# Weight gradient stage: who issues the row loads, and when the 3.2 MB operand is loaded

## The chip, the cores and the metric

One core of a Trainium2 chip. The metric is the device time of one execution in microseconds (us); times are medians of fast runs, and every run told here was fast (the single-look run, being alone, is of unknown state). A profile is one execution, so its span differs a little from the median.

## The reference, cut to what matters

The program is the backward pass of a block that adds segmented attention, gated by an MLP, to its input. Only the gradient of the attention weights Wq, Wk, Wv and of the attention's input concerns us here:

```python
q = jnp.einsum('btd,dhe->bhte', h, Wq)      # also k, v; 32 heads of 128, D = 640
scores = jnp.einsum('bhqe,bhke->bhqk', q, k) * scale
p = _softmax(jnp.where(mask, scores, -1e9))
o = jnp.einsum('bhqk,bhke->bhqe', p, v)
...
_out, _vjp = jax.vjp(_f, ...)               # gradients of all weights and of x
```

64 segments of 32 tokens and 8 memory tokens are handled three at a time: 22 units ("tl") of up to 120 rows.

## The kernel before: the parts concerned

The stage makes eight passes ("qd") over the 22 units, 512 weight columns a pass. For one unit it loads dS, P and the rows of output gradient ("g"), q and k. TensorE forms the three gradient blocks in PSUM (`s2`), ScalarE or VectorE copies them out, and `s4` multiplies them by the weights (the g matmuls, line 1390). After the 22 units, `wg` multiplies them by the layer's input rows `hr` (line 1411).

```python
def ld(u):                                        # five units ahead: NB = 5 buffers
    nc.sync.dma_start(dS[0:n], ...)
    nc.sync.dma_start(Pr[0:n], ...)
    for nm_ in ("g", "q", "k"):
        k.load_x(r, 0, src, nc.scalar if nm_ == "g" else nc.sync)   # token rows
        k.load_m(r, tl, nm_, c0, c0 + 512, nc.gpsimd)               # memory-token rows
...
def s2(u, i):
    ... four matmuls into pr ...
    if i == 0:   nc.scalar.copy(gr[0:n], pr[0:n])                   # line 1351
    elif i == 1: nc.vector.tensor_scalar(gr[0:n], pr[0:n], k.scale, ...)
    else:        nc.scalar.activation(gr[0:n], pr[0:n], ACT.Copy, scale=k.scale)   # line 1355
...
ld_to(2)
ld_w(0)                                           # three transposing weight loads, SyncE
ld_to(3)
nc.scalar.dma_start(hr[0:120], k.HRO[...])        # 3000 KB
nc.scalar.dma_start(hr[120:P], k.HRO[...])        # 200 KB
ld_to(5)
...
for qd in range(8):
    for p in range(NTL):                          # 22 units
        ...ld_to(u + 2 + NB); s2(u + 2, ...); s1(u + 3); s3(u + 1, ...); s4(u)
        if p == 4:
            spill(qd)                             # three loads gr<-GSP, 160 KB each, GpSimd
    ...
    for i in range(3):
        wg(qd, i)                                 # first reader of hr
```

In the traces of this stage ScalarE, SyncE and GpSimd run their instructions in the order in which the program wrote them. A DMA issue is one of these instructions; where one had to wait, what stood behind it in the same engine's queue waited too (8.46 us in the prediction's example). Two counts are in use below: the units that are loaded count from 0, as in the code, the places of the edits from 1 ("the seventh unit" is `u == 6`).

Of the kernel before, what the change touches and what calls it, by code (L numbers as in the profile page):

```python
# [16 lines left out]
P = 128  # L17
# [1247 lines left out]
def phase6_Awgrads(k, X, out0, out3, out4, out5):  # L1265

    nc, tc = k.nc, k.tc
# [4 lines left out]
    NF = NTL - 2  # L1272
# [5 lines left out]
    with tc.tile_pool(name="h6i", bufs=3) as io, tc.tile_pool(name="h6", bufs=1) as hp, \  # L1278
            tc.tile_pool(name="h6g", bufs=1) as gp, tc.tile_pool(name="h6a", bufs=1, space=bass.MemoryType.PSUM) as pa:
        start = len(nc.cur_bb.bb.instructions)  # L1280
        hr = hp.tile([P, NF, D], BF16, name="hr")
# [26 lines left out]
        def ld(u):  # L1308
            qd, tl = units[u]
            c0, h0 = qd * 512, qd * 4  # L1310
            ns, nm, nx, n = k.geo(tl)
            dS, Pr = dSs[u % NB], Prs[u % NB]
            nc.sync.dma_start(dS[0:n], k.DSR[tl][:, h0:h0 + 4, :])
            nc.sync.dma_start(Pr[0:n], k.PR[tl][:, h0:h0 + 4, :])
            rw = []
            for nm_ in ("g", "q", "k"):
                r = io.tile([120, 512], BF16, name="r6", tag=f"r6{nm_}", bufs=NB)
                src = k.g_src(tl, c0, c0 + 512) if nm_ == "g" else k.x_src(tl, nm_, c0, c0 + 512)
                k.load_x(r, 0, src, nc.scalar if nm_ == "g" else nc.sync)
                k.load_m(r, tl, nm_, c0, c0 + 512, nc.gpsimd)  # L1320
                rw.append(r)
            st["l", u] = (dS, Pr, rw)

        def ld_to(u):
            while cnt["l"] < min(u, len(units)):
                ld(cnt["l"])
                cnt["l"] += 1

        def s1(u):
            n = k.geo(units[u][1])[3]  # L1330
            dS = st["l", u][0]
            pt = pa.tile([P, 4, n], BF16, name="t6", tag=bank("x", 5, 3))
            for j in range(4):
                nc.tensor.transpose(pt[:, j, :], dS[0:n, j, 0:P], k.ident[0:n, 0:n])  # L1334
            nc.vector.tensor_copy(dSTs[u % 2][0:n, :, 0:n], pt[0:n])  # L1335

        def s2(u, i):
            qd, tl = units[u]
            n = k.geo(tl)[3]
            dS, Pr, rw = st["l", u]  # L1340
            lh = (Pr, dS, dSTs[u % 2])[i]
            pr = pa.tile([P, 512], F32, name="r6p", tag=bank("s", 3, 2))
            for j in range(4):
                nc.tensor.matmul(pr[:, j * P:(j + 1) * P], lh[0:n, j, :], rw[i][0:n, j * P:(j + 1) * P],  # L1344
                                 start=True, stop=True)
            if tl < NF:
                gr = grs[i][:, tl, :]
            else:
                gr = gp.tile([120, 512], BF16, name="grs", tag=f"grs{i}", bufs=2)[:]
            if i == 0:  # L1350
                nc.scalar.copy(gr[0:n], pr[0:n])  # L1351
            elif i == 1:
                nc.vector.tensor_scalar(gr[0:n], pr[0:n], k.scale, None, op0=ALU.mult)
            else:
                nc.scalar.activation(gr[0:n], pr[0:n], ACT.Copy, scale=k.scale)
            st["g", u, i] = gr
            if tl >= NF:
                r0 = 120 * (tl - NF)
                nc.gpsimd.dma_start(k.GSP[qd, i, r0:r0 + n, :], gr[0:n])  # L1359
            if i == 2:  # L1360
                st.pop(("l", u))

        def spill(qd):
            for i in range(3):
                nc.gpsimd.dma_start(grs[i][120:P, :, :], k.GSP[qd, i].rearrange("(t r) c -> r t c", r=8))

        def s3(u, i0, i1):
            qd, tl = units[u]
            nx = k.geo(tl)[2]
            a = (96 * tl) % R if tl < NF else R + 96 * (tl - NF)  # L1370
            pt = pa.tile([P, i1 - i0, 4, nx], BF16, name="t6g", tag=bank("x", 5, 3))
            for i in range(i0, i1):
                gr = st.pop(("g", u, i))
                for j in range(4):
                    nc.tensor.transpose(pt[:, i - i0, j, :], gr[0:nx, j * P:(j + 1) * P], k.ident[0:nx, 0:nx])  # L1375
            k.copy(ring[:, i0:i1, :, a:a + nx], pt[:], eng='s' if i1 == 2 else 'v')

        def s4(u):
            qd, tl = units[u]
            if tl < NF:  # L1380
                ws = [(w, P * (w % 3)) for w in range((96 * tl) // P, (96 * tl + 96) // P)]
            else:
                ws = [(NT - 1, R)] if tl == NF + 1 else []
            for w, r0 in ws:
                g = []
                for h in range(2):
                    pg = pa.tile([P, 320], F32, name="g6", tag=bank("g", 0, 3))
                    for i in range(3):
                        for j in range(4):
                            nc.tensor.matmul(pg[:], ring[:, i, j, r0:r0 + P], Ws[qd][i][:, j, 320 * h:320 * h + 320],  # L1390
                                             start=(i == 0 and j == 0), stop=(i == 2 and j == 3))
                    g.append(pg)
                gx = io.tile([P, D], BF16, name="gxo", tag="wgo", bufs=4) if qd == 7 else None
                for h in range(2):
                    a = acc[:, w, 320 * h:320 * h + 320]
                    if qd == 0:
                        nc.vector.tensor_copy(a, g[h][:])
                    else:
                        nc.vector.tensor_tensor(a if qd < 7 else gx[:, 320 * h:320 * h + 320], a, g[h][:], ALU.add)  # L1399
                if qd == 7:  # L1400
                    nc.sync.dma_start(k.GXA[P * w:P * w + P, :], gx[:])
# [16 lines left out]
        def out_ld(tt):  # L1418
            st["o"] = []
            for nm_, src in (("s", k.SR), ("g", k.GB), ("x", k.A_x)):  # L1420
                t_ = io.tile([P, D], BF16, name=f"eo_{nm_}", tag=f"eo_{nm_}", bufs=1)
                nc.gpsimd.dma_start(t_[:], src[tt * P:tt * P + P, :])
                st["o"].append(t_)

        def out_rows(tt):
            s, g, x = st.pop("o")
            nc.vector.tensor_tensor(g[:], s[:], g[:], ALU.mult)
            nc.vector.tensor_tensor(g[:], g[:], x[:], ALU.add)
            nc.gpsimd.dma_start(out0f[tt * P:tt * P + P, :], g[:])
# [16 lines left out]
        ld_to(2)  # L1446
        ld_w(0)
        ld_to(3)
        nc.scalar.dma_start(hr[0:120], k.HRO[0:120 * NF, :].rearrange("(t p) d -> p t d", p=120))
        nc.scalar.dma_start(hr[120:P], k.HRO[120 * NF:k.NR, :].rearrange("(t r) d -> r t d", r=8))  # L1450
        ld_to(5)
        for _ in head(0):
            pass
        for qd in range(8):
            u0 = NTL * qd
            for p in range(NTL):
                u = u0 + p
                if p + 2 < NTL:
                    ld_to(u + 2 + NB)
                    s2(u + 2, 0)  # L1460
                    s2(u + 2, 1)
                if p + 3 < NTL:
                    s1(u + 3)
                if p + 1 < NTL:
                    s3(u + 1, 0, 2)
                if p + 2 < NTL:
                    s2(u + 2, 2)
                if p + 1 < NTL:
                    s3(u + 1, 2, 3)
                s4(u)  # L1470
                if p == 4:
                    spill(qd)
                if p % 11 == 2:
                    out_ld(2 * qd + p // 11)
                if p % 11 == 6:
                    out_rows(2 * qd + p // 11)
            if qd < 7:
                ld_w(qd + 1)
                h = head(u0 + NTL)
            else:  # L1480
                xg = X.tile([P, NW * (D + 512)], BF16, name="xg", tag="x")
                gow = xg[:, 0:NW * D].rearrange("p (t d) -> p t d", d=D)
                orr = xg[:, NW * D:NW * (D + 512)].rearrange("p (t d) -> p t d", d=512)
                h = NW // 2
                for a in range(2):
                    rows = slice(h * P * a, h * P * (a + 1))
                    nc.scalar.dma_start(gow[:, h * a:h * a + h, :], k.GWO[rows, :].rearrange("(t p) d -> p t d", p=P))
                    nc.sync.dma_start(orr[:, h * a:h * a + h, :], k.OR[rows, 0:512].rearrange("(t p) c -> p t c", p=P))
            for i in range(3):
                wg(qd, i)  # L1490
                if qd < 7:
                    next(h)
# [337 lines left out]
def kernel(  # L1830
# [42 lines left out]
    with tc.tile_pool(name="xw", bufs=1) as X:  # L1873
        wo_ops = phase6_Awgrads(k, X, out_0, out_3, out_4, out_5)
        phase5_Bbwd_ln(k, X, *wo_ops, out_1, out_6, out_7, out_8, out_9)
# [35 lines left out]
```

## Time and profile before

| | before |
|---|---|
| median, range | 5483.78 us, 5476.4 to 5496.66 (3 runs when the prediction was made; with a fourth, 5476.62, the median is 5480.2) |
| span of the profiled run | 5474.2 us |
| TensorE busy | 88% of the span |
| the stage (end of the chain before it to the end of the last wg) | 1420 us |

Busy time and share of each engine, from the page, then TensorE's work in the first and second pass (columns: window, its length, TensorE busy and its matmuls, granted clock, share of the DMA engines busy, GB/s):

```profile
PE 4830.6 (88%) x66012; PEld 3050.2 (56%) x66012; DVE 2297.2 (42%) x7285; ACT 1752.0 (32%) x4913; POOL 1558.4 (28%) x2673
...
3424.00:3553.00 129.00, 93.09 (x993) 0.82 0.70 160
3624.00:3725.00 101.00, 89.92 (x983) 0.95 0.64 156
```

The first pass has about the same work as the second, yet takes 28 us longer. A pass of 101 us leaves TensorE idle for 11. Whatever is to be gained in this stage lies in those differences, and in the time for which the clock is below 1. The waits behind them stand in the prediction.

### The profile page before, as it was taken

The numbers are of one execution on the slowest core, as the hardware profiler recorded it, in microseconds if no ns is written. First come the engines' busy times: TensorE is split into PE (matmuls) and PEld (weight loads), VectorE is DVE, ScalarE is ACT, GpSimd is POOL, SyncE is SP. The second block draws the span as 40 slices with busy tenths as digits, with TensorE's granted clock in tenths as the row PEclk, the third lists the DMA queues.
The fourth block names the chain that finished last, engine by engine and source line by source line (L and its number), as shares of the span: only waits on it lengthen the run. The fifth ranks groups of instructions, "written<-read, shape, count | busy, mean of one in ns | idle before, by whom it ended". The sixth has DMA issues, their size and how long they took to land. (4 is left out here: it accounts for less than half of the span.)

```text
span 5474.2 us, 163087 instructions
## 1 busy us (share of the span) xinstructions
PE 4830.6 (88%) x66012; PEld 3050.2 (56%) x66012; DVE 2297.2 (42%) x7285; ACT 1752.0 (32%) x4913; POOL 1558.4 (28%) x2673
## 2 busy tenths in 40 slices
PE   4988899989999785999999998789998999999999
PEld 2544555555555443555666665555566555666665
DVE  5833555555555423444444443322233222311451
ACT  2422455555555422232333332222233222301111
POOL 0000334343444212333333332432344333310100
PEclk9998999999999787999999999899999999999999
DMA  7553455555544587666766664744355444657332
GB/s 248 177 188 91 134 154 159 154 159 156 159 154 149 131 190 156 175 185 173 194 182 179 185 184 111 164 113 96 96 134 124 111 106 97 167 178 184 111 111 94
DMA packets 1004358, 822.92 MB, mean 150 GB/s; under 512 B 507009, under 2 KB 892333, under 8 KB 1000929
## 3 DMA queue, kind: packets, MB, share of 16 engines
q1 hardware_dynamic: 758779, 559.22, 37.2%
q0 software_dynamic: 95696, 155.10, 10.3%
q10 hardware_dynamic: 149130, 98.17, 6.5%
q8 instruction: 521, 8.54, 0.7%
q14 instruction: 232, 1.90, 0.1%
HBM read 476.95 MB, written 303.09 MB: 142 GB/s over the span
## 5 line engine op out<-in xcount | busy, mean ns | idle before, releaser
L1411 PE MATMUL wg<-gr,hr 128*128 128x512 bf16 x2400 | 529.4, 382 | 16.1 <-DVE dST L1335 12.9
L1390 PE MATMUL g<-w,ghacc 128*128 128x320 bf16 x3072 | 456.8, 307 | 0.0
L1411 PEld LDWEIGHTS <-hr 128*128 128x128 bf16 x2400 | 235.5, 98 | 301.5 <-issue 27.3
L1390 PEld LDWEIGHTS <-ghacc 128*128 128x128 bf16 x3072 | 301.9, 100 | 120.1
L308 PEld LDWEIGHTS <-hx 128*32 128x32 bf16 x7680 | 180.0, 97 | 170.0 <-issue 13.7
L90 DVE CAST wgo<-wg 128x512 bf16<-128x512 f32 x72 | 47.5, 687 | 524.5 <-issue 268.1
L90 DVE CAST stg<-bank 128x512 bf16<-128x512 f32 x256 | 177.0, 691 | 208.9 <-PE bank L308 197.2
L327 PEld LDWEIGHTS <-gkv 128*8 128x8 bf16 x8192 | 189.8, 87 | 109.1 <-DVE gkv L1002 24.6
L611 ACT ACTIVATE xP<-xsp,xnm 120x120 bf16<-120x120 f32 (+1 forms) x704 | 240.0, 375 | 8.7 <-DVE xnm L607 5.4
L660 POOL DMA_DIRECT2D OR<-xv x163 | 92.7, 569 | 470.5 <-ACT xv L659 347.7
L1154 POOL DMA_DIRECT2D DSR<-gdS x176 | 101.0, 574 | 434.7 <-DVE gdS L1152 410.7
L92 ACT CAST wgo<-wg 128x512 bf16<-128x512 f32 x48 | 25.8, 589 | 572.0 <-PE wg L1411 572.0
L1351 ACT CAST gr<-r6p 120x512 bf16<-120x512 f32 x160 | 93.8, 586 | 357.5 <-PE r6p L1344 255.3
L1223 PE MATMUL gbank<-WqT,ident 128*128 128x512 bf16 x640 | 204.8, 404 | 0.0
L622 POOL TENSOR_TENSOR xP<-xP,xrz 120x480 bf16<-120x480 bf16 x163 | 161.7, 992 | 136.1 <-ACT xP L611 96.1
L1399 DVE TENSOR_TENSOR ghacc<-ghacc,g 128x320 f32<-128x320 f32 x192 | 93.5, 487 | 244.7 <-PE g L1390 244.7
L1152 DVE SCALAR_TENSOR_TENSOR gdS<-gdp,Dx,gPr 120x120 bf16<-120x120 f32 (+1 forms) x680 | 182.8, 330 | 0.0
L245 POOL DMA_DIRECT2D r<-GOS x256 | 144.0, 566 | 130.1 <-PE r6p L1344 92.1
L1359 POOL DMA_DIRECT2D GSP<-grs x48 | 25.6, 539 | 534.6 <-ACT grs L1351 517.4
L308 PE MATMUL gbank<-WoT,gox 128*32 128x512 bf16 x2560 | 153.6, 386 | 24.2 <-POOL gox L957 20.9
L327 PE MATMUL bank<-Wo,oTm 128*32 128x320 bf16 x4032 | 170.2, 320 | 0.1
L1123 POOL DMA_DIRECT2D VTD<-gvT x176 | 130.6, 744 | 137.1 <-ACT gvT L1122 115.8
(342 smaller groups left out, 11150.4 us busy)
## 6 DMA issues: line engine op xcount, KB each, us to landing
QVS<-stg SPq DMA_DIRECT2D x128, 256.0 KB
gqv<-QVS SPq DMA_DIRECT2D x108, 192.0 KB
vTt<-VTD SPq DMA_DIRECT2D x64, 320.0 KB
VTD<-gvT POOLq DMA_DIRECT2D x168, 120.0 KB, 3.6
DSR<-gdS POOLq DMA_DIRECT2D x168, 120.0 KB, 3.5
dS<-DSR SPq DMA_DIRECT2D x168, 120.0 KB
P<-PR SPq DMA_DIRECT2D x168, 120.0 KB
gPr<-PR SPq DMA_DIRECT2D x164, 120.0 KB
```

Source lines behind the costliest of these rows:

```text
L90: return nc.vector.tensor_copy(out, in_)
L245: eng.dma_start(d, src if src.shape[0] > 1 else src[0])
L308: k.nc.tensor.matmul(bank[32 * g:32 * g + 32, :], x[:, dc, :], W[:, dc, c0:c0 + 512], start=(dc == 0), stop=(dc == k.DC - 1), tile_positio ...
L327: k.nc.tensor.matmul(pm[p0:p0 + nq, 0:320], x[:, h, :], W[:, h, 320 * b:320 * b + 320], start=(first and i == 0), stop=(last and i == 15), ...
L611: nc.scalar.activation(Pb[0:n, j, 0:n], sp[0:n, j, :], ACT.Exp, bias=nmx[0:n, j:j + 1], scale=k.scale, accum_out=Z[0:n, j:j + 1])
L622: eng.tensor_tensor(Pb[0:n, :, 0:n], Pb[0:n, :, 0:n], bc_last(rz[0:n], n), ALU.mult)
L1123: nc.gpsimd.dma_start(k.VTD[tl][:, :, h0:h0 + 4, :], vTq[:])
L1152: nc.vector.scalar_tensor_tensor(dS[0:n, j, 0:n], dp[0:n, j, :], Dx[0:n, j:j + 1], Pr[0:n, j, 0:n], op0=ALU.subtract, op1=ALU.mult)
L1154: nc.gpsimd.dma_start(k.DSR[tl][:, h0:h0 + 4, :], dS[0:n])
L1223: nc.tensor.matmul((bA if g in ("W1", "G1", "G2") else bB)[:], k.ident[:], WqT[:, 0, 0:512], start=True, stop=True)
L1390: nc.tensor.matmul(pg[:], ring[:, i, j, r0:r0 + P], Ws[qd][i][:, j, 320 * h:320 * h + 320], start=(i == 0 and j == 0), stop=(i == 2 and j ...
L1411: nc.tensor.matmul(accs[dc][:], hr[:, tl, dc * P:(dc + 1) * P], grs[i][:, tl, :], start=(tl == 0), stop=(tl == NF - 1))
```

## The change

The intent: ScalarE should issue no row loads in the stage, so that its copies out of PSUM never stand behind a waiting DMA; and the big load of `hr`, needed only at the end of the first pass, should not be the first thing that the stage asks of the DMA engines.

```diff
-                k.load_x(r, 0, src, nc.scalar if nm_ == "g" else nc.sync)
+                k.load_x(r, 0, src, nc.sync)
...
         ld_to(3)
-        nc.scalar.dma_start(hr[0:120], k.HRO[0:120 * NF, :].rearrange("(t p) d -> p t d", p=120))
-        nc.scalar.dma_start(hr[120:P], k.HRO[120 * NF:k.NR, :].rearrange("(t r) d -> r t d", r=8))
         ld_to(5)
...
                 if p == 4:
                     spill(qd)
+                if u == 6:
+                    nc.sync.dma_start(hr[0:120], k.HRO[0:120 * NF, :].rearrange("(t p) d -> p t d", p=120))
+                    nc.sync.dma_start(hr[120:P], k.HRO[120 * NF:k.NR, :].rearrange("(t r) d -> r t d", r=8))
```

## The prediction

> **What bounds the kernel now.** I read the page first, then TensorE's waits in the weight gradient stage, then ScalarE's, then the timeline at the places where the long ones lie. In the page TensorE is busy for 88% of the span and the other four engines for 42% or less, so time is to be had only where TensorE stands still. Its waits from 3380 to 4860 us, which hold the stage (columns: engine, line, releaser: us in total, times, longest):
>
> ```profile
> PE r6p L1344 <- ACT gr L1351: 46.0, 12, 7.2
> PE r6p L1344 <- ACT grs L1351: 34.1, 13, 27.5
> PE r6p L1344 <- ACT gr L1355: 19.4, 27, 0.8
> PE t L1334 <- DMA r<-GOS: 10.4, 1, 10.4
> PE r6p L1344 <- DMA r<-QVS: 5.9, 5, 3.2
> ```
>
> The first two lines say that TensorE waits for ScalarE's copy out of PSUM. ScalarE is busy for a quarter of this stage, so the copies are not too slow; something holds them. ScalarE's own waits in the same stretch:
>
> ```profile
> ACT gr L1351 <- DMA r<-GOS: 52.2, 11, 8.5
> ACT grs L1351 <- DMA r<-KX: 41.9, 1, 41.9
> ACT gr L1351 <- DMA P<-PR: 12.2, 2, 6.9
> ACT gr L1351 <- DMA r<-KS: 10.7, 3, 5.4
> ACT gr L1351 <- DMA r<-GX: 10.1, 4, 2.5
> ```
>
> A copy PSUM to SBUF needs no DMA. It waits for one because a DMA issue stands before it in ScalarE's queue and that issue waits. The timeline of the fourth of the eight column passes shows one (start, duration, what, in brackets the idle time before it):
>
> ```profile
> 3998.72 0.60 ACT L1355 ACTIVATE gr<-r6p 120x512 bf16<-120x512 f32 x1
> 4007.43 0.31 ACTq L267 DMA_DIRECT2D r<-GOS  x1
> 4007.78 0.58 ACT L1351 CAST gr<-r6p 120x512 bf16<-120x512 f32 x1 [8.46 <-DMA r<-GOS]
> ...
> 4008.42 0.58 PE L1344 MATMUL r6p<-r,dST 120*128 120x128 bf16 x4 [5.44 <-ACT gr L1351]
> ```
>
> ScalarE stood for 8.46 us with the issue of an output gradient row load at the head of its queue; the cast ran straight after it, and TensorE after the cast. Each pass has such a place, where the spill loads (gr<-GSP) crowd the DMA engines. What the issue waits for I took from the instruction list of the kernel before as compiled: SyncE's and ScalarE's DMAs share eight semaphores in turn, and each DMA waits until the one eight issues earlier has landed. Slow landings therefore block the issuer, and whatever compute is queued behind it.
>
> The second place is the start of the stage:
>
> ```profile
> 3412.70 0.38 ACTq L1449 DMA_DIRECT2D hr<-HRO  x1
> 3425.08 0.28 ACTq L1450 DMA_DIRECT2D hr<-HRO  x1
> 3450.51 0.86 ACTq L267 DMA_DIRECT2D r<-GOS  x2
> 3451.41 0.58 ACT L1351 CAST grs<-r6p 120x512 bf16<-120x512 f32 x1 [41.94 <-DMA r<-KX]
> ...
> 3435.50 0.31 SPq L267 DMA_DIRECT2D r<-KS  x1
> 3435.85 2.91 SPq L272 DMA_TRANSPOSE w<-in_A_Wv_dram  x1
> ...
> SPq L267 <- DMA hr<-HRO: 19.2, 1, 19.2
> ...
> 3420.00:3436.00 16.00, 1.41 (x11) 0.86 (x9) 1.10 (x2) 0.00 (x0) 7.11 (x13) 0.50 0.97 178
> ```
>
> The reader is to see that the 3.2 MB hr load goes first, fills the DMA engines (share 0.97, 178 GB/s) until about 3435.5, and that SyncE waits 19.2 us for its semaphore before it may issue the weight transposes and the rows of units 2 to 5. ScalarE's issues for units 3 and 4 then wait for those. TensorE does 90 us' work in 129 us of the first pass, against about 90 in 101 of the second; hr's first reader, wg, starts only at 3552.8.
>
> **What the Trainium skill says.** DMA: Bandwidth & Descriptors, section "Anatomy of one DMA": a semaphore wait is made by the issuing sequencer before dispatch, not by the DMA engine. The trace agrees, with 8.46 us before an issue of 0.31 us. The same page, "Issuing engines are not separate DMA queues": transfers from all issuers run on the same 16 engines, and several issuers save only issue time. So the change frees no bandwidth, and hr is as expensive later as early. Same page, "Queues, rings and completion order": within one issuer's queue each DMA engine takes descriptors in ring order. Before, hr sat in ScalarE's queue, so this trace cannot show it; after, unit loads issued behind it on SyncE should start after it. TensorE: Matmul & The Clock Gate, "What's actually happening": after an idle window of about 3.4 us the clock falls to half. The trace agrees: granted clock 0.50 from 3420 to 3452, and the four-matmul group that takes 0.38 to 0.39 us in steady state takes 0.58 after the wait of 5.44.
>
> **The change part by part.**
> (a) The 176 issues of output gradient rows leave ScalarE. By its own duration (median 0.31 us) that is 55 us of ScalarE's sequencer time, but off the path, since they lie under its running activations; I count nothing. What counts is that the casts are no longer held. For passes two to eight, TensorE's waits window by window on gr L1351 are 2.9, 7.2, 5.7, 6.6, 5.0, 7.1 and 6.8, and in the second pass the 3.2 us put down to r<-QVS ends with the same kind of late cast: 44.5 us together. After each, about 3 to 6 us of work runs at half clock (a g group of 24 matmuls 4.17 against 3.43, each small group 0.2 more), some 1.5 us a pass, 10 in all. I take the whole 55 as gain, since the data should be there in time: unit u+6 is requested when unit u+1's buffers come free and needed some four units of 4 us later, 16 us, while landings take 3.5 us (median), and at most 14.
> (b) SyncE gains the same 176 issues. Five a unit at about 0.43 us with overhead are 2.2 us, of 4 to 5 us per unit: it keeps up. No cost.
> (c) Start without hr. SyncE begins at 3412.8 as before. Ten loads at 0.43 end by about 3417.3; three transposes at 2.8 end at 3425.7 (before: 3444.24, so 18.5 earlier). Units 2 to 4, now with the output gradient rows, take 15 issues or 6.5 us, and 3 us for the last to land: 3435. The first g group of matmuls then starts at about 3438, against 3461.2. This is 23 us earlier; I book 22.
> (d) hr in the seventh unit. On SyncE it follows the loads of unit 12 and precedes those of unit 13. In a pass like the fourth the last of unit 12 is issued about 14.5 us after the fifth unit begins (4006.6 against 3992.1), because the spill slows landings. hr takes 3.28 MB at 177 GB/s, 18.5 us, and with the company of other loads I put it at 20, then 3 for unit 13: landed 37.5 us after that mark. TensorE needs unit 13 at about the tenth unit, some 25 after the mark. So a new wait of about 12.5 us, 2.5 of paced loads after it and 2 at half clock: 17. It replaces this pass's own waits at the spill (4.8 and 1.5 of clock, 6.5 rounded up). Net cost 10.
> Sum: 55 + 22 - 10 = 67 us gained. 5483.78 - 67 = 5417.
>
> **The rivals.** First, the wait only changes its name: the casts go freely, but the same late landings now hold SyncE, and TensorE waits for rows instead of casts. For it: SyncE too has waits on landings, and five DMAs a unit now pass one in-order queue with eight in flight. Against it: the four units of slack, and that today's landings are on time by the time the casts are freed (waits on row DMAs apart from the start and the misnamed 3.2 are under 4 us). If half of (a) goes this way, the gain is about 40: 5444. Second, hr hurts in the middle as much as at the start: its transfer occupies the same engines for 20 us with the five-unit reserve as the only cover, the spill's congestion is just over, and the queue is now one. If unit 13 is late by 30 rather than 12.5, the gain is 50: 5434. Third, hr is hidden altogether by the reserve, and SyncE, no longer coupled to ScalarE's late issues through the shared semaphores, runs further ahead: gain 67 + 15, perhaps 85: 5399. Fourth, nothing moves because TensorE is at its limit anyway; the idle time of about 150 us in gaps between 3409 and 4765 speaks against it.
>
> **Range and chances.** The change touches only one stage of about 1410 us and can return no more than its idle and half-clock time, some 160 us; 2% is 110 us. For that the casts, the start and the middle would all have to come out far better than worked out: 0.04. For a loss of 110 the hr wait would have to be ten times my figure: 0.01. The first two rivals together give about 5450, the third 5399, runs scatter by about 10 us each way. I predict 5417, with 8 chances in 10 from 5390 to 5448.
>
> **What would show it.** ScalarE's waits L1351 <- DMA should vanish from passes two to eight, and TensorE's wait on ACT gr L1351 fall from 46 to under 8 us, with no row wait of like size in its place (right for (a), else the first rival). Passes two to eight should shorten from about 102 to about 94 us each. The first g matmul should start near 3438. The hr issue should lie near 3455 to 3465, and 15 to 20 us later there should be one wait of 8 to 20 us on rows or dS in the first pass; if it is absent the third rival is right, if over 25 the second. wg of the first pass should begin 8 to 18 us earlier than 3552.8. The prediction is wrong if time moves outside this stage.

## The result, and the profile after

The changed kernel took 5400.14 us (5392.24 to 5407.13, 4 runs) beside 5480.2 us; the ratio is 0.9848, 95% interval 0.9822 to 0.9873. By the limit of 2% that is "same", but clear of noise. A ratio here is the mean time of one kernel's runs over that of the other's in the same rounds, so it is not quite the ratio of the medians quoted.

TensorE's waits in the stage (3380 to 4790 us), then ScalarE's, of the changed kernel:

```profile
PE t L1334 <- DMA dS<-DSR: 29.7, 7, 16.6
PE r6p L1344 <- ACT gr L1355: 19.5, 27, 0.8
PE r6p L1344 <- ACT grs L1351: 6.3, 13, 0.6
```

```profile
ACT gr L1351 <- PE r6p L1344: 294.7, 120, 9.2
...
ACT grs L1351 <- DMA r<-KS: 7.9, 1, 7.9
```

The line that led before, TensorE waiting 46.0 us for ACT gr L1351, is gone, and so are ScalarE's waits for DMAs ahead of that cast. The one that is left (7.9 us, at the start) is TensorE's own lack of rows: the cast waits for a matmul that waits for a load. A new line leads, the wait for dS, and its longest piece is 16.6 us. The timeline shows where it comes from (SyncE, then TensorE, changed kernel):

```profile
3460.88 0.43 SPq L1472 DMA_DIRECT2D hr<-HRO  x1
3461.35 6.36 SPq L1473 DMA_DIRECT2D hr<-HRO  x1
3467.81 2.53 SPq L1313 DMA_DIRECT2D dS<-DSR  x1
...
3474.03 0.75 SPq L1313 DMA_DIRECT2D dS<-DSR  x1
3484.54 0.32 SPq L1314 DMA_DIRECT2D P<-PR  x1
...
3469.19 0.39 PE L1344 MATMUL r6p<-r,dS 120*128 120x128 bf16 x4
3486.15 0.58 PE L1334 MATMUL t<-ident,dS 120*128 120x120 bf16 x4 [16.57 <-DMA dS<-DSR]
```

The dS of unit 13 is issued 7 us after hr, and TensorE has it 18 us later. SyncE itself stands from 3474.78 to 3484.54: it has issued seven DMAs after the big one, and the eighth (the P of unit 14) shares its semaphore with hr. So hr has landed 23.7 us after its issue. The start of the stage, in the changed kernel:

```profile
3399.68 0.82 PE L1223 MATMUL gbank<-WqT,ident 128*128 128x512 bf16 x3
3406.98 0.56 PE L1334 MATMUL t<-ident,dS 120*128 120x120 bf16 x4 [6.48 <-DMA r<-GOS]
...
3420.99 0.58 PE L1334 MATMUL t<-ident,dS 120*128 120x120 bf16 x4 [7.78 <-DMA dS<-DSR]
...
3430.77 4.80 PE L1390 MATMUL g<-w,ghacc 128*128 128x320 bf16 x24
```

```profile
3408.38 2.54 SPq L272 DMA_TRANSPOSE w<-in_A_Wv_dram  x1
3410.97 3.12 SPq L272 DMA_TRANSPOSE w<-in_A_Wk_dram  x1
3414.13 3.26 SPq L272 DMA_TRANSPOSE w<-in_A_Wq_dram  x1
3417.43 0.59 SPq L1313 DMA_DIRECT2D dS<-DSR  x1
```

The first g group comes 31 us after the last matmul of the chain before, against 52. What is left of the start is the 9 us for which the three transposes occupy SyncE ahead of unit 2's dS. And the passes from the first wg to the end of the stage, before and after (columns as above; here with the busy time of weight loads, VectorE, ScalarE and GpSimd in between):

```profile
3552.80:4829.00 1276.20, 1165.79 (x9402) 744.59 (x9399) 369.19 (x786) 311.16 (x510) 430.67 (x776) 0.95 0.46 114
```

```profile
3534.50:4754.20 1219.70, 1151.38 (x9401) 736.56 (x9399) 369.11 (x786) 310.31 (x510) 430.57 (x776) 0.97 0.49 119
```

TensorE's idle time falls from 110.4 to 68.3 us (length less busy), 42.1; the same matmuls are also 14.4 us shorter, which fits the granted clock, 0.97 instead of 0.95. Together that is 56.5.

I take four instants from each trace: the start of the last warm-up matmul (line 1223) of the chain before the stage, the first g matmul, the first wg and the end of the last wg. They split the stage into the three terms of the prediction. For all kernels:

| kernel (one profile each) | start to first g | first g to first wg | first wg to end | stage |
|---|---|---|---|---|
| before | 52.4 | 91.6 | 1276.2 | 1420.1 |
| changed | 30.7 | 103.7 | 1219.8 | 1354.1 |
| changed, again | 30.0 | 103.5 | 1214.2 | 1347.7 |
| rows only | 49.3 | 86.1 | 1219.1 | 1354.5 |
| hr only | 28.0 | 110.5 | 1289.7 | 1428.2 |
| changed, hr on ScalarE | 29.9 | 101.1 | 1215.4 | 1346.4 |
| changed, hr on GpSimd | 28.4 | 102.1 | 1217.3 | 1347.8 |
| changed, hr in the thirteenth unit | 30.2 | 98.7 | 1216.0 | 1344.8 |
| changed, hr spread | 29.7 | 89.2 | 1215.8 | 1334.7 |
| hr spread, rows first | 23.9 | 93.5 | 1216.0 | 1333.4 |
| before, late spill (timed run) | 52.0 | 89.2 | 1256.0 | 1397.2 |
| changed, late spill | 30.2 | 96.8 | 1217.2 | 1344.2 |
| spread, rows first, late spill | 24.1 | 92.7 | 1217.6 | 1334.3 |

The stage is the better measure here. The stages ahead of it run the same instructions in all these kernels, except for at most three row issues at their very end, and still the stage began anywhere from 3395 to 3429 us in the profiles. That scatter goes into every total.

### The profile page after: what moved, and what is told of

Same layout as the page of the kernel before. It is cut to its first block, busy times and chain, and to the rows that moved or that the text cites. A ratio compares the mean times of both kernels' runs of the same rounds, so it can differ in the third digit from the quotient of the medians.

```text
span 5405.4 us, 163107 instructions
## 1 busy us (share of the span) xinstructions
PE 4823.1 (89%) x66012; PEld 3045.0 (56%) x66012; DVE 2298.6 (43%) x7285; ACT 1750.8 (32%) x4913; POOL 1558.0 (29%) x2673
## 5 line engine op out<-in xcount | busy, mean ns | idle before, releaser
L1154 POOL DMA_DIRECT2D DSR<-gdS x176 | 101.1, 575 | 428.5 <-DVE gdS L1152 410.0
L1351 ACT CAST gr<-r6p 120x512 bf16<-120x512 f32 x160 | 93.9, 587 | 295.8 <-PE r6p L1344 294.7
L92 ACT COPY ghacc<-t6g 128x768 bf16<-128x768 bf16 (+1 forms) x176 | 137.1, 779 | 106.0 <-PE t6g L1375 102.7
```

Of the source, the lines that this page charges most:

```text
L92: return nc.scalar.copy(out, in_)
```

## The experiments

They ran in three sessions, each with its own runs of the kernel before on the same chip: 5480.33 us in the first (c0, e1, e2, e4), 5475.45 in the second (e3, e5, e6, e7), 5473.23 in the third (e6b, e8, e9, e10). All results were correct.

My theory: the gain is the sum of casts set free (passes two to eight and the first pass's spill) and an earlier start, less a new wait behind hr. The rivals: the waits only change their names; or the early hr load was what mattered; or the DMA engines are simply full in the first pass and no order of issue helps.

**c0, the changed kernel again.** No edit.

> The changed kernel itself, once more, on the chip of the parts below. By the profiles its gain lies in the stage alone: first g group of matmuls 21.7 us sooner after the stage's start, the first pass 12.1 us longer after that, passes two to eight with their wg 56.4 us shorter, 66 us together. Expected 5400 to 5415 beside 5480; anything over 75 us of gain is not explained by the stage's three terms.

Measured: 5415.05 us, ratio 0.9875 (0.9849 to 0.9902), stage 1347.7. By medians the gain is 65 us here and was 80 the first time, while the stage gained 72 and 66 in the two profiles. The stage accounts for the change; what the first 80 had over it is within the scatter of the rest.

**e1, rows only.** The kernel before with one line of the change:

```diff
-                k.load_x(r, 0, src, nc.scalar if nm_ == "g" else nc.sync)
+                k.load_x(r, 0, src, nc.sync)
```

> Output gradient rows by SyncE, hr as before, first and on ScalarE. My theory (terms add up): the 55 us of passes two to eight and the 6 of the first pass's spill are gained, plus some 5 us at the start, since the first casts no longer stand behind row issues; hr still holds SyncE there for 19 us. About 66 us gained, 5415: as good as the whole change, the hr move being worth about nothing net. First rival (the wait only changes its name): gain of 30 or less.

Measured: 5413.41 us, ratio 0.9875 (0.9853 to 0.9898): the same as the whole change in the same session. The passes after the first are as short as in the changed kernel (1219.1). The first pass is short too (86.1), since nothing large lies in it, but the start is still long (49.3). TensorE's waits from 3416 to 3552 us show what hr at the start costs when the casts no longer stand behind it:

```profile
PE r6p L1344 <- DMA r<-GX: 19.5, 2, 12.0
PE t L1334 <- DMA dS<-DSR: 16.2, 4, 8.4
```

So the wait on ScalarE did change its name at the start, into waits for rows. In the later passes it did not, and that is where the gain lies. The first rival falls.

**e2, hr only.** The changed kernel with the row line put back:

```diff
-                k.load_x(r, 0, src, nc.sync)
+                k.load_x(r, 0, src, nc.scalar if nm_ == "g" else nc.sync)
```

> hr in the seventh unit on SyncE, output gradient rows still by ScalarE. My theory: 22 us gained at the start, 17 lost in the middle, and some 5 more there because ScalarE's row issues behind hr hold the casts; ScalarE's holds at the spills stay, TensorE's wait on ACT gr L1351 stays over 40 us. Gain 0 to 10 us, 5470 to 5484. A rival in which the early hr load is what matters most expects 20 us or more of gain.

Measured: 5477.79 us, ratio 1.0003 (0.9967 to 1.0038). The start is 24 us shorter and the first pass 19 us longer; later passes gain nothing. The casts are held even more, as TensorE's waits of the stage tell:

```profile
PE r6p L1344 <- ACT gr L1351: 57.7, 19, 7.5
```

That the early hr load was what mattered is refuted: moving it alone is worth nothing: what the start gains (24 us) the first pass loses (19 us). (Its stage, 1428.2, is even 8 us longer than before in this one profile, in which the run was also the slowest of its four; the ratio is the better witness.)

**e4, hr spread over the pass.** The changed kernel with

```diff
-                if u == 6:
-                    nc.sync.dma_start(hr[0:120], ...)          # 3000 KB
-                    nc.sync.dma_start(hr[120:P], ...)          # 200 KB
+                if u in (6, 9, 12, 15, 18):
+                    h0 = 4 * ((u - 6) // 3)
+                    nc.sync.dma_start(hr[0:120, h0:h0 + 4, :],
+                                      k.HRO[120 * h0:120 * h0 + 480, :].rearrange("(t p) d -> p t d", p=120))
+                if u == 11:
+                    nc.sync.dma_start(hr[120:P], ...)
```

> The changed kernel with hr in five pieces of 4 tiles (600 KB) in units 7, 10, 13, 16 and 19, and its last 8 partitions in unit 12, all on SyncE. My theory: the 16.6 us wait for dS is the one large load ahead of the unit loads in SyncE's queue; a piece of 600 KB is one unit's worth (3.4 us) and the reserve of four units covers it, so the wait falls under 3 us and 15 to 18 us are gained on the changed kernel: about 5385. Rival (the DMA engines are simply full in the first pass, whatever the order): the wait is only spread, less than 6 us gained.

Measured: 5397.59 us, ratio 0.985 (0.9827 to 0.9872), 17 us below the changed kernel's median of the same session (its four runs lie between 5391.68 and 5407.65, the changed kernel's between 5404.8 and 5417.33); the first pass took 89.2 us instead of 103.5. TensorE's waits of the first pass, in the changed kernel (c0) and then here:

```profile
PE t L1334 <- DMA dS<-DSR: 17.1, 1, 17.1
```

```profile
PE t L1334 <- DMA dS<-DSR: 2.9, 2, 2.5
```

and the first pass of this kernel in one window (columns as in the result; the last three are clock, DMA share and GB/s):

```profile
3443.00:3533.00 90.00, 83.49 (x908) 66.36 (x906) 41.35 (x91) 35.58 (x57) 50.01 (x90) 0.96 0.96 194
```

The DMA engines are busy for 96% of this pass and TensorE hardly waits. Full engines alone did not cause the wait, so the rival by which no order of issue helps falls. What caused it is 3.2 MB asked for at one place. The five pieces also lie further apart, and five pieces issued at one place were not tried: whether the length of one transfer ahead of the unit loads counts, or so many bytes in so short a time, e4 does not tell.

**e3 and e9, hr from another queue.** The changed kernel, still in the seventh unit, with both hr issues on ScalarE (e3) or on GpSimd (e9):

```diff
-                    nc.sync.dma_start(hr[0:120], ...); nc.sync.dma_start(hr[120:P], ...)
+                    nc.scalar.dma_start(hr[0:120], ...); nc.scalar.dma_start(hr[120:P], ...)   # e3; e9: nc.gpsimd
```

> The changed kernel with both hr issues on ScalarE instead of SyncE, still in the seventh unit. Same bytes at the same time, another queue. My theory (unit loads stand behind hr in SyncE's queue): beside hr instead of behind it they land sooner, the wait for dS falls from about 17 to under 10 us, though ScalarE's casts may be held some 5 us by its second hr issue; stage 5 to 10 us shorter than the changed kernel's 1348 to 1354. Rival (the engines are full, order does not matter): wait on rows, dS and casts together stays 15 us or more and the stage stays at 1348 to 1354.

> The changed kernel with both hr issues on GpSimd, in its own queue and holding no compute, still in the seventh unit. If the loads behind hr wait because they stand in the same queue, the wait for dS (SyncE's loads) falls under 8 us, and what waits instead are the memory-token rows that GpSimd itself issues behind hr (r, 5 to 15 us). If the DMA engines are simply full, dS waits as long as now, 15 us or more. The time itself 5395 to 5410 in both.

Measured: e3 5404.57 us, ratio 0.9871 (0.9854 to 0.9887), stage 1346.4; e9 5417.58 us, ratio 0.9897 (0.9873 to 0.9921), stage 1347.8 (e9's time lies 8 us above the stretch expected of it). Neither is distinguishable from the changed kernel. In e3 the 17 us wait for dS is gone, and this stands in its place (ScalarE, then TensorE):

```profile
3467.04 0.60 ACT L1355 ACTIVATE gr<-r6p 120x512 bf16<-120x512 f32 x1
3474.03 0.39 ACTq L1472 DMA_DIRECT2D hr<-HRO  x1
3480.44 1.62 ACTq L1473 DMA_DIRECT2D hr<-HRO  x1
3482.10 0.59 ACT L1351 CAST gr<-r6p 120x512 bf16<-120x512 f32 x1 [14.46 <-issue]
...
3482.74 0.59 PE L1344 MATMUL r6p<-r,dST 120*128 120x128 bf16 x4 [13.45 <-ACT gr L1351]
```

Two issues at the head of ScalarE's queue held it for 14.46 us: the disease of the kernel before, in one dose, and nearly three times what I had expected of it. In e9 it is GpSimd's queue that stands; its waits from 3420 to 3560 us, then TensorE's next matmul:

```profile
POOL r L245 <- DMA hr<-HRO: 19.8, 1, 19.8
```

```profile
3486.83 0.34 PE L1375 MATMUL t6g<-ident,gr 96*128 96x96 bf16 x4
3501.96 0.58 PE L1344 MATMUL r6p<-r,P 120*128 120x128 bf16 x4 [14.79 <-DMA dS<-DSR]
```

The wait of 14.8 us comes at the matmul that reads P and the rows of a unit, no longer at the transpose of dS that came first in the changed kernel. It ends 1.3 us after GpSimd's does (3500.68). The profile names dS as the releaser, but this matmul does not read dS; I take it for the memory-token rows that stood behind hr, which fits the times and is not shown. In each case the loads or the compute of the queue that took hr are what runs late, with a wait of 13 to 17 us. Whether SyncE's loads were slowed less by hr beside them than by hr ahead of them is not settled: in e3 unit 13's dS had been issued before hr, and in e9 SyncE's issues stall as well.

**e5 and e8, hr or the spill elsewhere.** The changed kernel with one number altered each:

```diff
-                if u == 6:
+                if u == 12:          # e5: hr later
```

```diff
-                if p == 4:
+                if p == 12:          # e8: spill later, hr still at u == 6
                     spill(qd)
```

> The changed kernel with both hr loads in the thirteenth unit. My theory: the seventh unit is a bad place since the spill of the fifth has eaten SyncE's lead by then; in the thirteenth the lead of four units (16 to 17 us) is whole when hr's 20 us and 3 for the next unit begin, so the wait is 5 to 8 us instead of 17 and the stage about 1340. Rival (lead does not matter, one large load costs its own length): wait stays at 15 or more.

> The changed kernel with the spill after unit 13, hr still in the seventh unit. My theory (step d of the prediction): the spill eats SyncE's lead before hr; without it hr is issued sooner against TensorE's progress and the wait for dS falls from 17 to about 9 to 11 us, as with hr in unit 13. Passes two to eight should not change, since nothing holds the casts there: 5 to 8 us gained on the changed kernel. Rival (the lead is not what counts): wait stays 15 or more.

Measured: e5 5399.93 us, ratio 0.9866 (0.9851 to 0.9881), and the longest wait for dS is 11.0 us; e8 5403.23 us, ratio 0.9885 (0.9856 to 0.9915), longest wait 8.0. The first pass is 98.7 and 96.8 us against 103.5 to 103.7. So the spill just ahead of hr does cost part of the lead, 6 to 9 us of the wait and 5 to 7 us of the pass; in the totals this is inside the noise, as the overlapping intervals say. e5 came out 3 us over the wait that I had expected.

**e6 and e6b, the late spill in the kernel before.**

```diff
-                if p == 4:
+                if p == 12:
                     spill(qd)
```

> The kernel before with the spill loads of each pass after unit 13 instead of unit 5. My theory: it is the spill's crowding that makes landings slow and ScalarE's row issues hold the casts; so TensorE's wait on ACT gr L1351 stays (35 to 55 us in all) but lies in the second half of each pass. Rival (the holds come from something at a pass's start, such as the out rows or the stores of the pass before): the waits stay near the sixth unit.

> The kernel before with the spill after unit 13, timed now: the single look gave 5442 and TensorE's wait on ACT gr L1351 fell to 18.8 us from 46.0 instead of staying. If the holds are set by how far the row loads lag when the spill comes (more at unit 5, so soon after the pass's start), this repeats: waits of 15 to 25 us and 20 to 30 us gained, 5450 to 5460. If the one look was luck: 5475.

Measured: one look at 5441.85 us; then 20 runs, 5452.28 us (5437.18 to 5464.19), ratio 0.996 (0.9949 to 0.9971). TensorE's waits on the casts in the timed kernel's profile:

```profile
PE r6p L1344 <- ACT gr L1351: 17.0, 11, 3.7
```

The place was foretold rightly by e6: the longer holds now lie in the second half of each pass, as at 4197.3 us in the pass from 4133.7 to 4232.2, so it is the spill that brings them about. The size was not: 18.8 and then 17.0 us instead of 46.0, where e6 expected 35 to 55. e6b's own figures came true, but no run tests the reason that it gives (how far the row loads lag).

The traces show two differences. First, ScalarE is held less: its waits of the cast for DMAs (the lines `ACT gr L1351 <- DMA`) sum to 73 us instead of 100, and the longest is 6.8 instead of 8.5. Second, a hold costs TensorE less. Here is one of the kernel before, then that of the pass above (ScalarE, then TensorE):

```profile
3837.78 0.58 ACT L1351 CAST gr<-r6p 120x512 bf16<-120x512 f32 x1 [7.56 <-DMA r<-GOS]
...
3828.95 0.34 PE L1375 MATMUL t6g<-ident,gr 96*128 96x96 bf16 x4
3829.12 0.39 PE L1344 MATMUL r6p<-r,P 120*128 120x128 bf16 x4
...
3838.42 0.58 PE L1344 MATMUL r6p<-r,dST 120*128 120x128 bf16 x4 [7.21 <-ACT gr L1351]
```

```profile
4200.06 0.31 ACTq L267 DMA_DIRECT2D r<-GX  x1
4200.41 0.58 ACT L1351 CAST gr<-r6p 120x512 bf16<-120x512 f32 x1 [6.44 <-DMA r<-QVS]
...
4192.88 3.42 PE L1390 MATMUL g<-w,ghacc 128*128 128x320 bf16 x24
4196.14 0.39 PE L1344 MATMUL r6p<-r,P 120*128 120x128 bf16 x4
...
4201.05 0.58 PE L1344 MATMUL r6p<-r,dST 120*128 120x128 bf16 x4 [3.75 <-ACT gr L1351]
```

By the program one unit in four has no g matmuls. Of a hold of over 4 us TensorE loses all but 0.35 us right behind such a unit, where it runs out of work sooner; behind a unit with its 24 g matmuls (3.4 us) it loses 2.7 to 3.0 us less than the hold, and twice in the kernel before nothing at all. Of the kernel before's holds of over 4 us, five are of the first kind (7.56, 6.91, 5.33, 6.88 and 5.58 us) and cost 30.5 of the 46.0 us. With the late spill all eight are of the second kind. Counting also the waits behind a late cast that the profile puts down to a DMA, TensorE loses 27.5 us instead of 49.0, and the difference is about what was gained. Why the late spill puts the holds at other units is not shown. The single number is worth having all the same: one moved line in the kernel before gives 20 us, about a third of the change.

**e7 and e10, towards a better version.** e7 is e4 with the rows of all five units ahead of the weights at the start; e10 is e7 with the late spill.

```diff
-        ld_to(2)
-        ld_w(0)
-        ld_to(3)
         ld_to(5)
+        ld_w(0)
```

> hr spread in five pieces, and at the start of the stage all five units' rows before the weight transposes. The transposes hold SyncE 9 us, during which units 2 to 4 wait (7.8 us of TensorE's wait in the spread version); the weights are first needed after unit 4's rows. Expected: first g group 27 us after the stage's start instead of 30, so 0 to 4 us gained on the spread version, about 5392 beside 5397. If the weights become what is waited for, 0.

> hr spread, rows before weight transposes at the start, and the spill after unit 13: all that was found together. Against the spread version with rows first (5389): 0 to 5 us gained, as no cast is held any more and only the first pass's small waits on rows remain. If late spills also relieve the passes two to eight, up to 20 us.

Measured: e7 5389.22 us, ratio 0.9843 (0.9825 to 0.9861), stage 1333.4; e10 5386.55 us, ratio 0.9849 (0.983 to 0.9868), stage 1334.3. In e7 the first g group comes 6 us sooner and the pass is 4 us longer, with a new line among TensorE's waits:

```profile
PE g L1390 <- DMA w<-in_A_Wv_dram: 4.4, 1, 4.4
```

The weights became what is waited for, the second branch of the expectation. The late spill adds nothing once no cast can be held. All of e4, e7 and e10 beat the kernel before, with ratios of 0.9843 to 0.985 on their own sessions' runs of it; among themselves they are equal. That they also beat the changed kernel is shown by the runs for e4 alone, in its session; for e7 and e10 it rests on the stage (1333 to 1334 us beside 1348 to 1354), since the changed kernel's own ratios were 0.9848 and 0.9875 and it was not run beside them.

## Why the prediction was right

The time on record was 5417 with a range of 5390 to 5448; measured were 5400.14 and, in a later session, 5415.05. The sum was 67; by medians the gain was 80 and 65. The terms, against the two profiles of the changed kernel:

| term | predicted | first profile | second profile |
|---|---|---|---|
| (a) passes two to eight | 55 gained | 56.4 | 62.0 |
| (c) start | 22 gained | 21.7 | 22.4 |
| (d) first pass, net | 10 lost | 12.1 | 11.9 |
| sum | 67 | 66.0 | 72.5 |

(a) The casts set free. Right, in mechanism and size: the holds vanish, no row wait of like size replaces them, and a pass from the end of one wg to the start of the next falls from 101.5 to 93.4 us on average, where 94 was foretold. Of its two parts the half-clock work was put too low (10 us; TensorE's busy time fell by 14.4) and the idle time a little too high (44.5 against 42.1). That the total fits to 2 us is therefore partly luck.

(b) SyncE keeps up. Right: five issues a unit leave no row wait in the passes after the first among TensorE's leading ones, and SyncE's lead of four units covers the spill.

(c) The start. Right to within a microsecond as an interval (22 booked, 23 worked out). As an instant, the first g at 3438, it came at 3430.8, because this run reached the stage 8.7 us sooner. (The 90 us of work that the prediction reads in the 129 us from 3424 are 93.1 in the line shown; no term rests on it.)

(d) hr in the seventh unit. The new wait is there, once, for the dS of unit 13, after the spill and behind hr in SyncE's queue, as worked out; 16.6 and 17.1 us rather than 12.5. From the beginning of the fifth unit (3442.39 us in the first profile), hr is issued after 18.5 us where 14.5 was assumed, has landed 23.7 later instead of 20, and unit 13 is there after 43.8 instead of 37.5; TensorE stands for it from 27.2, not 25. So the terms that were mis-sized are the issue of hr, 4.0 us late, and its transfer, 3.7 us too short. The second could have been read from the prediction's own lines: hr was issued at 3412.70, and the SyncE issue that waited for it ran at 3435.50, 22.8 us later. The 2.5 us of paced loads that were added on top did not show as waits, so that the net came out within 2 us; this is luck. The instant of hr's issue (3460.88) lies inside the stretch foretold only because the run reached the stage 8.7 us sooner: counted from the stage's start it comes some 5 us after the latest time foretold. Counted so, the first wg came 9.6 us earlier than before, within the 8 to 18.

The rivals. "The wait only changes its name" is right for the start alone, as e1 shows, and wrong for the passes. "hr is hidden altogether" is wrong, and so is a middle wait above 25 us. That time would move outside the stage was named as what would refute me; the stages outside scatter by up to some 30 us from profile to profile, so nothing smaller in a single pair can be read there. In the pair that was predicted, the time outside is 4054.1 us before and 4051.3 after: the stage alone explains the gain of the profiles.

One reading of the sum was too generous. The prediction books 22 less 10, or 12 us, to the move of hr. e1 shows that with the rows on SyncE the move brings nothing measurable (ratio 0.9875 with and without it; stage 1354.5 without, 1354.1 and 1347.7 with it). The 6.5 us of the first pass's own spill that were set against the new wait, and some 3 us of the start, come with the row line alone.

## What to carry to other kernels

Keep DMA issues that may have to wait out of the queue of an engine whose next instruction is on the path: the 55 us of an engine's issue time were worth nothing here, the few places where an issue waited in front of a cast were worth about 56. Moving the large load away from the start did not make it cheaper (0.9875 with and without the move); cutting it into five pieces spread over the pass took its longest wait from 17.1 to 2.5 us. To judge a change in one stage, take the stage's own instants from several traces rather than one pair of totals.

## What the Trainium skill lacked or had wrong

- DMA: Bandwidth & Descriptors, "Issuing engines are not separate DMA queues", says that several issuers only save the time of issuing. It lacks the other side: which engine issues decides which compute stands behind a waiting issue. The row line alone, which changes just the issuer, gave 0.9875.
- The same page, "Anatomy of one DMA", gives about 2 us plus bytes over 436 GB/s for one DMA that GpSimd issues, which for hr (3.28 MB) is an estimate of 9.5 us. Beside the unit loads hr took 25.2 us from issue to the release of the waiting issuer when GpSimd issued it (e9), and 23.7 when SyncE did. The page has no figure for a large load among others.
- The same page has no figure for how long an issue can occupy the issuing sequencer under load: hr's second issue (200 KB) took 6.36 us on SyncE and the dS behind it 2.53, where SyncE's issues of unit loads in this kernel have medians of 0.30 to 0.40.
